# FNet mixing with a GeGLU feed-forward block: GpSimd's tensor work is given to VectorE

## The chip, the cores and the metric

The kernel runs on one core of one Trainium2 chip. The core has a tensor engine (PE, with a separate row PEld for the loading of weights), a vector engine (DVE, called VectorE or `V` in the code), a scalar engine (ACT, `A`), a general-purpose engine (POOL, GpSimd or `G`), and SP, whose queue issues all of this kernel's DMA transfers. Each engine executes its own instructions in the order in which they were written; semaphores make it wait for others. PE, DVE, ACT and POOL meet in SBUF; PE's results lie in PSUM banks. The metric is the device time of one execution in microseconds; less is better. Durations below come from one profiled execution.

## The reference

With tokens S = 2048, width D = 448 and inner width DF = 1792, all in float32:

```python
a = einsum("bsd,ed->bse", layernorm(x), dft_hid_re)
b = einsum("bsd,ed->bse", layernorm(x), dft_hid_im)
h = x + einsum("ts,bse->bte", dft_seq_re, a) - einsum("ts,bse->bte", dft_seq_im, b)
g = einsum("bsd,df->bsf", layernorm(h), w_gate)
u = einsum("bsd,df->bsf", layernorm(h), w_up)
out = h + einsum("bsf,fd->bsd", gelu(g) * u, w_down)
```

The layernorms have no affine part (eps 1e-5), the gelu is the tanh approximation.

## The kernel before

**Numbers in halves.** PE works in float16. Every operand is split into a hi part (made by ACT, `hi_part`, L108) and a lo part, the rest that hi leaves (made by DVE, `lo_part`, L112 and L114). A product takes several float16 matmuls. Many of the matrix products are Strassen-like: seven products of sums and differences of quarter blocks instead of eight. The sums of quarters (`..._sums`) are side work for DVE or POOL, and each result then gets its hi and lo part.

**Stages.** The sequence transform takes 64 steps; in steps 32 to 63 it is done by seven products ("fast", from about 175 to 333 us). In between, the hidden transform and the weights are prepared. Then the feed-forward block runs over three blocks of tokens: block 0 with 1024 tokens (14 tiles t = 0 to 13, about 334 to 460 us, "the gate/up block" below), and blocks 1 and 2 with 512 tokens each (tiles 14 to 41, 460 to 663 us), into which the down projection is woven (`dn_mm`). A tail of down products follows (663 to 695 us). A tile is one pair of quarter columns of gate and up: 38 matmuls of 512 columns in block 0, of 256 columns later.

**One gate/up tile** (class `GateUp`) has seven products in the banks X, Y, Z. Their names in the profile: `m` is a scaled copy of Z, `u` one of Y, `g` the gelu of X (all by ACT). DVE's `plus` (L1179) adds `u` to Z and gives `c` (c12 in the code); a second `plus` (L1179) adds `m` to Y and writes one half of `hs`, the hidden tile. Only then may PE add the last product y3 into Y. y3 of tile t is issued after the first two products of tile t+1, so that DVE has this long to do c and hs of tile t. From Y after y3, DVE makes the other half of `hs` by a product with `g` (L1248). ACT applies the gelu to `c` (L1261), and POOL multiplies that into the first half of `hs` (L1263, the gated product). Then SP stores `hs` (L1269) into a DRAM tile (`hid_dram`), from where the down projection loads it again as `hid` (L1286). `hs` has two buffers. In block 0 the sums of such loads are `dn_s` (L1333 to L1335), their hi and lo parts `dn_w`.

**Side work by slots.** Everything else in the gate/up block (gate/up weights for later tiles, the weights of down, normalised tokens for blocks 1 and 2) is hung on numbered slots: three per step of the sequence transform, then eight per tile from slot 192 on. `do(q)` emits what the tables put on slot q, at that place in the order of all engines. The tables: `W_AT` (gate/up weights: load, sums, hi, lo, store), `P_AT` (hidden transform and the moments of h), `F_AT` and `H_AT` (norms, sums, hi, lo and transposes of h), `T_AT` (sums of the transform's operands), `D_AT` (weights of down: load, sums, hi, lo in two pieces). A number in a table thus sets which instruction of DVE stands ahead of which. `gu_w` and `gw` are gate/up weights; their store into DRAM is L400, their load L1277; `wd` is a tile of down's weights, `wd_s` its five sums (L232 to L235, POOL), `xs` and `tt` belong to the normalised tokens, `hops` to their transposed form (SP's DMA transposes, L327).

**POOL's other work.** After each pair of token tiles of h, `ffn_rstd` refines a reciprocal square root: DVE's reciprocal, then five small steps on POOL (L213 to L217); `ffn_bias` has one more (L240) for four tiles. When a pair of token tiles is done in the down projection, class `Drain` adds PE's banks into `hr`: three adds straight from PSUM by DVE (L1111) and eight sums (L1139) with copies `v` made by ACT (L1107). In the loop these sums are given to DVE, in the tail (drains 5 and 6) they take the default engine, POOL. The last drain adds from PSUM (L1588) and its stores end the kernel.

Of the kernel before, what the change touches and what calls it, by code (L numbers as in the profile page):

```python
# [11 lines left out]
ALU = mybir.AluOpType  # L12

P = 128
S, D, DF = 2048, 448, 1792
# [7 lines left out]
EPS = 1e-5  # L23


X_SC = 16.0
# [6 lines left out]
def kernel(  # L33
# [173 lines left out]
    def ffn_rstd(q, j):  # L207
        tag = f"h{q}_{j}"
        mv = moments[q, j]
        sd = root(mv, tag, D)  # L210
        r = const.tile([P, 4, 2], F32, tag=f"r_{tag}", name=f"r_{tag}")
        V.reciprocal(r[:, 0], sd)
        G.tensor_scalar(r[:, 1], mv[:, :, 1], D * EPS, -0.5 / (D * X_SC**2), op0=ALU.add, op1=ALU.mult)  # L213
        G.tensor_mul(r[:, 2], r[:, 0], r[:, 0])
        G.tensor_mul(r[:, 2], r[:, 2], r[:, 1])
        G.tensor_scalar(r[:, 2], r[:, 2], 1.5, None, op0=ALU.add)
        G.tensor_mul(r[:, 3], r[:, 2], r[:, 0])  # L217
        moments[q, j] = mv, r[:, 3]


# [7 lines left out]
    def down_sums(n):  # L228
        t = wd32[n]
        place = (late, "dn_s") if n > 1 else (fops, "xs")  # L230
        s = wd_s[n] = place[0].tile([P, 5, HD], F32, tag=place[1], name=f"wd_s_{n}")
        G.tensor_sub(s[:, 2:4], t[:, 0:2], t[:, 2:4])  # L232
        t22 = t.rearrange("p (a b) d -> p a b d", a=2)
        G.tensor_add(s[:, 0:2], t22[:, :, 0], t22[:, :, 1])
        G.tensor_add(s[:, 4], t[:, 0], t[:, 3])  # L235

    def ffn_bias(q, j):
        mv, r = moments[q, j]
        if q < 2:
            G.tensor_mul(mv[:, :, 1], mv[:, :, 0], r)  # L240
            return
        sign = -1.0 if (q, j) == (NB - 1, 1) else 1.0
        V.scalar_tensor_tensor(mv[:, :, 1], mv[:, :, 0], sign, r, op0=ALU.mult, op1=ALU.mult)
# [537 lines left out]
    def h_store(q, j):  # L781
# [3 lines left out]
    gu, gw = {}, {}  # L785
    W_AT = {
# [14 lines left out]
    }  # L801
    P_AT = {
# [7 lines left out]
    }  # L810
    F_AT = {
# [4 lines left out]
    }  # L816
    T_AT = {
        6: (41, 46, 48),
        7: (48, 50, 54),
        0: (50, 54, 54),  # L820
        1: (57, 61, 63),
        2: (68, 92, 94),
        3: (67, 92, 93),
        4: (65, 68, 70),
        5: (69, 72, 72),
    }
    H_AT = {
# [4 lines left out]
    }  # L832
    D_AT = {
# [259 lines left out]
    class Drain:  # L1093
# [27 lines left out]
        def bank3(self):  # L1121
            self.add(3, 6, 1.0)

        def sums(self, parts, E=G):
            x11, x12, x21, x22 = self.x
            M3, M4, M2, M5 = self.v
            ops = (
                (E.tensor_add, x12, M3),
                (E.tensor_sub, x21, M4),
                (E.tensor_add, x21, M2),  # L1130
                (E.tensor_add, x12, M5),
                (E.tensor_sub, x11, M4),
                (E.tensor_add, x22, M3),
                (E.tensor_sub, x11, M5),
                (E.tensor_sub, x22, M2),
            )
            for k in parts:
                op, x, m = ops[k]
                op(x, x, m)  # L1139
# [46 lines left out]
    class GateUp:  # L1186
# [58 lines left out]
        def y3(self):  # L1245
            self.mul(self.Y, "A22", "T4", False)
            h, y, g = self.hidden(0), self.cols(self.Y), self.cols(self.g1)
            V.scalar_tensor_tensor(h, y, SC, g, op0=ALU.mult, op1=ALU.mult)  # L1248

        def cols(self, a):  # L1250
            return a.rearrange("p (n t) -> p n t", t=P)
# [7 lines left out]

        def c_last(self):  # L1260
            A.activation(self.c12, self.c12, AF.Gelu_apprx_tanh, scale=1.0 / H_SC)  # L1261
            c22 = self.hidden(1)
            G.tensor_mul(c22, c22, self.cols(self.c12))  # L1263

        def store(self):

# [146 lines left out]
    for t in range(NF):  # L1413
# [46 lines left out]
        if t == 3:  # L1460
            mv = moments[NB - 1, 1]
# [190 lines left out]
```

## Time and profile before

| | |
|---|---|
| time, median of 3 runs | 697.32 us (696.77 to 698.31) |
| profiled execution | 697.04 us, of which span 695.2 us, granted clock 1.000 |
| PE | 687.0 us busy, 99% of the span |
| DVE | 575.9 us, 83%, 1203 instructions |
| ACT | 416.9 us, 60% |
| POOL | 113.8 us, 16%, 127 instructions |
| gate/up block, 392 to 452 us | DVE 52.07 of 60 us, ACT 42.76, POOL 25.60 |

A row of a group reads: line, engine, operation, output<-inputs, shapes, how often | busy us in total, mean ns of one | idle time of the engine just before, and what ended it. A row of waits reads: who waited at which line <- for whom: us in total, how often, the longest. A row of the timeline reads: start, duration in us, engine, line, operation, count, and in brackets the idle time before it with what ended it; several like instructions in a row are put together. Idle time of an engine other than PE costs nothing by itself, unless PE waits behind it.

### The profile page before, as it was taken

How to read it: one execution, taken by the hardware profiler on the slowest of the kernel's cores; microseconds unless marked ns; L12 is line 12 of the kernel's file. 1: busy time of each engine (PE TensorE's matmuls, PEld its weight loads, DVE VectorE, ACT ScalarE, POOL GpSimd, SP SyncE). 2: the span in 40 equal slices, each digit the busy share in tenths (PEclk: the TensorE clock that was granted, in tenths of full speed). 3: DMA queues.
4: the chain of work that ended last, by engine and by line, in shares of the span. 5: the costliest groups of instructions: out<-in, count | busy, mean ns of one | idle time of the engine just before them, and what ended most of it. 6: DMA issues, size and time to landing. Idle time of an engine off the chain costs nothing.

```text
span 695.2 us, 13978 instructions
## 1 busy us (share of the span) xinstructions
PE 687.0 (99%) x5266; PEld 509.4 (73%) x5266; DVE 575.9 (83%) x1203; ACT 416.9 (60%) x855; POOL 113.8 (16%) x127
## 2 busy tenths in 40 slices
PE   9999999999999999999999999999999999999998
PEld 5555555555979889987644444459999999999997
DVE  7999799879999898995548997867788876899786
ACT  5777665957766655555536867655555453655631
POOL 0000001010011001000033443511020111233224
DMA  8778659879957649583655679697989985787612
GB/s 288 251 226 283 158 208 253 294 203 293 225 184 182 188 114 207 173 217 141 159 196 189 230 261 291 202 307 245 258 225 288 295 286 184 294 300 276 242 47 81
DMA packets 115781, 155.43 MB, mean 224 GB/s; under 512 B 63744, under 2 KB 80256, under 8 KB 115712
## 3 DMA queue, kind: packets, MB, share of 16 engines
q1 hardware_dynamic: 115712, 154.53, 73.3%
q8 instruction: 41, 0.67, 0.4%
q14 instruction: 28, 0.23, 0.1%
HBM read 105.74 MB, written 34.34 MB: 201 GB/s over the span
## 4 chain that ended last, share of the span: by engine, by line
PE 91%; DVE 3%; DMA 3%; ACT 1%; issue 1%; SPq 0%; DVEq 0%; ACTq 0%
PE acc L682 21%; PE acc_f L560 19%; PE acc_d L1373 15%; PE pY L1169 12%; PE y L768 9%; PE pZ L1169 8%; PE pX L1169 8%; DVE gu_w L114 1%; DMA hid_dram<-hs 1%; DMA gw<-w_dram 1%; ACT gu_w L108 0%; DMA x<-in_x_dram 0%; SPq L327 0%; ACT u L1225 0%; DVE hs L1179 0%
## 5 line engine op out<-in xcount | busy, mean ns | idle before, releaser
L1169 PEld LDWEIGHTS <-gw 128*128 128x128 f16 x1330 | 129.9, 98 | 44.1 <-issue 2.9
L682 PE MATMUL acc<-xs,ws 128*128 128x448 f16 x768 | 146.4, 352 | 0.1
L560 PEld LDWEIGHTS <-ws 128*128 128x128 f16 x1344 | 128.8, 98 | 1.6
L682 PEld LDWEIGHTS <-ws 128*128 128x128 f16 x768 | 75.1, 98 | 70.2 <-ACT ws L108 0.2
L1373 PE MATMUL acc_d<-wd,dn_w 128*128 128x224 f16 x1008 | 110.9, 259 | 1.7 <-DVE dn_w L112 1.7
L1373 PEld LDWEIGHTS <-dn_w 128*128 128x128 f16 x1008 | 96.7, 98 | 4.2 <-DVE dn_w L112 2.1
L1263 POOL TENSOR_TENSOR hs<-hs,c 128x256 f32<-128x256 f32 (+1 forms) x42 | 60.5, 1439 | 230.0 <-ACT c L1261 186.6
L560 PE MATMUL acc_f<-t,ws 128*128 128x224 f16 x768 | 91.9, 259 | 0.0
L1169 PE MATMUL pY<-hops,gw 128*128 128x256 f16 (+1 forms) x560 | 85.6, 294 | 1.9 <-DVE hs L1179 1.5
L114 DVE SCALAR_TENSOR_TENSOR ws<-wr,ws 128x768 f16<-128x768 f32 (+2 forms) x66 | 69.8, 1058 | 10.1 <-ACT ws L108 10.1
L560 PE MATMUL acc_f<-xs,ws 128*128 128x224 f16 x576 | 73.5, 259 | 0.0
L108 ACT ACTIVATE ws<-wr 128x768 f16<-128x768 f32 (+2 forms) x66 | 60.5, 916 | 10.2 <-DMA wr<-in_w_seq_dram 9.1
L768 PE MATMUL y<-wh,z 128*128 128x448 f16 x336 | 66.2, 352 | 0.0
L1169 PE MATMUL pX<-hops,gw 128*128 128x256 f16 (+1 forms) x385 | 61.7, 294 | 0.0
L1169 PE MATMUL pZ<-hops,gw 128*128 128x256 f16 (+1 forms) x385 | 61.7, 294 | 0.0
L768 PEld LDWEIGHTS <-z 128*128 128x128 f16 x336 | 32.9, 98 | 29.3
L1179 DVE SCALAR_TENSOR_TENSOR c<-pZ,u 128x256 f32<-128x256 f32 (+1 forms) x42 | 21.4, 508 | 36.6 <-ACT dn_w L108 17.7
L1214 ACT ACTIVATE pY<-pX 128x256 f32<-128x256 f32 (+1 forms) x42 | 18.4, 439 | 53.9 <-PE pX L1169 50.4
L108 ACT ACTIVATE ws<-sums 128x512 f16<-128x512 f32 x64 | 38.5, 623 | 18.6 <-DVE sums L510 14.2
L1169 PEld LDWEIGHTS <-gu_w 128*128 128x128 f16 x266 | 25.9, 98 | 31.3 <-issue 0.3
L1225 ACT ACTIVATE u<-pY 128x256 f32<-128x256 f32 (+1 forms) x42 | 19.0, 454 | 45.0 <-PE pY L1169 44.7
L112 DVE TENSOR_TENSOR dn_w<-dn_s,dn_w 128x640 f16<-128x640 f32 x48 | 42.0, 874 | 1.6 <-ACT dn_w L108 1.6
(160 smaller groups left out, 980.0 us busy)
## 6 DMA issues: line engine op xcount, KB each, us to landing
gw<-w_dram SPq DMA_DIRECT2D x35, 896.0 KB, 6.9
wr<-in_w_seq_dram SPq DMA_DIRECT2D x100, 256.0 KB, 4.3
hid_dram<-hs SPq DMA_DIRECT2D x27, 512.0 KB, 7.0
hid<-hid_dram SPq DMA_DIRECT2D x54, 256.0 KB, 5.3
w_dram<-gu_w SPq DMA_DIRECT2D x14, 896.0 KB, 4.8
wr<-in_w_seq_dram SPq DMA_DIRECT2D x14, 512.0 KB, 4.9
gu_raw<-in_w_gu_dram SPq DMA_DIRECT2D x14, 384.0 KB, 5.6
gu_raw<-in_w_gu_dram SPq DMA_DIRECT2D x14, 320.0 KB, 5.0
```

Source lines behind the costliest of these rows:

```text
L108: A.activation(dst, src, AF.Copy, scale=scale)
L112: V.tensor_sub(dst, src, hi)
L114: V.scalar_tensor_tensor(dst, src, scale, hi, op0=ALU.mult, op1=ALU.subtract)
L560: PE.matmul(fast_sum(n, k), fast_a(n, i, lw, a), fast_b(j, lx, b), start=j == 0 and m == 0 and k in (0, 1, 3, 5), stop=j == NT // 2 - 1 an ...
L682: PE.matmul(acc[key][:, :D], w[:, lw, block * P : (block + 1) * P], xs[c][:, lx, :], start=c == 0 and m == 0, stop=c == NT - 1 and m == 2,)
L768: PE.matmul(y[:, :D], z[p][:, lz, k, g * P : (g + 1) * P], wh[:, lw, k, :], start=p == NP - 1 and k == 0 and m == 0, stop=k == 6 and m == ...
L1169: PE.matmul(ps, w[:, wo, :], ops[:, OPS[b] + m, :], start=first and n == 0, stop=last and n == len(W_TERMS[a]) - 1, skip_group_check=True,)
L1179: V.scalar_tensor_tensor(dst, ps, SC, other, op0=ALU.mult, op1=ALU.add)
L1214: A.activation(self.Y, self.X, AF.Copy)
L1225: A.activation(self.u2, self.Y, AF.Copy, scale=SC)
L1263: G.tensor_mul(c22, c22, self.cols(self.c12))
L1373: PE.matmul(ps, w[:, la, a, :], wd[n][:, lb, b, :], start=n == 0 and m == 0 and opens, stop=n == NC - 1 and m == 2, skip_group_check=True,)
```

## The change

Five kinds of work leave POOL for DVE: the gated product, which now stands in `y3` behind the product with `g` (L1249 in the changed code; it stood in `c_last`); the three sums of each tile of down's weights; the small steps of `ffn_rstd`, of which two are now one; the product in `ffn_bias`; and the drain sums of the tail. POOL keeps the memsets and the identity matrix. The tables get other numbers at some places. One line less at L216 shifts all later lines by one.

```diff
@@ ffn_rstd
-        G.tensor_scalar(r[:, 1], mv[:, :, 1], D * EPS, -0.5 / (D * X_SC**2), op0=ALU.add, op1=ALU.mult)
-        G.tensor_mul(r[:, 2], r[:, 0], r[:, 0])
-        G.tensor_mul(r[:, 2], r[:, 2], r[:, 1])
-        G.tensor_scalar(r[:, 2], r[:, 2], 1.5, None, op0=ALU.add)
-        G.tensor_mul(r[:, 3], r[:, 2], r[:, 0])
+        V.tensor_scalar(r[:, 1], mv[:, :, 1], D * EPS, -0.5 / (D * X_SC**2), op0=ALU.add, op1=ALU.mult)
+        V.tensor_mul(r[:, 2], r[:, 0], r[:, 0])
+        V.tensor_mul(r[:, 2], r[:, 2], r[:, 1])
+        V.scalar_tensor_tensor(r[:, 3], r[:, 2], 1.5, r[:, 0], op0=ALU.add, op1=ALU.mult)
@@ down_sums
-        G.tensor_sub(s[:, 2:4], t[:, 0:2], t[:, 2:4])
+        V.tensor_sub(s[:, 2:4], t[:, 0:2], t[:, 2:4])
...
-        G.tensor_add(s[:, 0:2], t22[:, :, 0], t22[:, :, 1])
-        G.tensor_add(s[:, 4], t[:, 0], t[:, 3])
+        V.tensor_add(s[:, 0:2], t22[:, :, 0], t22[:, :, 1])
+        V.tensor_add(s[:, 4], t[:, 0], t[:, 3])
@@ ffn_bias
-            G.tensor_mul(mv[:, :, 1], mv[:, :, 0], r)
+            V.tensor_mul(mv[:, :, 1], mv[:, :, 0], r)
@@ tables
-        11: (1, 37, 46, 48, 51, 51, 51, 54, 54, 58),
+        11: (1, 39, 48, 48, 51, 51, 51, 54, 54, 58),
...
-        0: (49, 45, 51, 58, 61, 62, 64),
-        1: (62, 60, 66, 68, 73, 75, 76),
+        0: (50, 46, 52, 59, 61, 62, 64),
+        1: (62, 60, 66, 70, 75, 77, 76),
...
-        5: (259, 260, 268, 273, 273, 274, 276, 276, 281, 284, 284, 289, 285, 289, 285, 293),
+        5: (253, 254, 262, 267, 267, 268, 270, 270, 281, 284, 284, 289, 285, 289, 285, 293),
...
-        0: (192, 195, 203, 204, 203, 206, 206),
-        1: (187, 213, 217, 217, 218, 221, 221),
-        2: (207, 229, 233, 233, 234, 237, 237),
-        3: (223, 245, 249, 249, 250, 253, 253),
+        0: (184, 197, 203, 204, 201, 207, 207),
+        1: (187, 215, 219, 219, 220, 223, 226),
+        2: (206, 228, 232, 232, 233, 236, 237),
+        3: (229, 245, 249, 250, 251, 254, 254),
...
@@ Drain
-        def sums(self, parts, E=G):
+        def sums(self, parts, E=V):
@@ GateUp.y3
             V.scalar_tensor_tensor(h, y, SC, g, op0=ALU.mult, op1=ALU.mult)
+            c22 = self.hidden(1)
+            V.tensor_mul(c22, c22, self.cols(self.c12))
@@ GateUp.c_last
             A.activation(self.c12, self.c12, AF.Gelu_apprx_tanh, scale=1.0 / H_SC)
-            c22 = self.hidden(1)
-            G.tensor_mul(c22, c22, self.cols(self.c12))
```

How this moves instructions is shown at three places of the gate/up block. First, DVE from the moments of h's last token tile (L205) to hs of tile 3, before:

```order
L205 BN_AGGR mv_h_1_4512<-st_h_1_1_4606 128x2
L1248 SCALAR_TENSOR_TENSOR hs_4572<-pY_4474,g_2_4557 128x4x128
L114 SCALAR_TENSOR_TENSOR wd_4261<-wd_1_4166,wd_4261 128x448
L1179 SCALAR_TENSOR_TENSOR c_3_4651<-pZ_4597,u_3_4631 128x512
L1179 SCALAR_TENSOR_TENSOR hs_4653<-pY_4582,m_3_4603 128x4x128
L114 SCALAR_TENSOR_TENSOR wd_4261<-wd_s_4593,wd_4261 128x448
L114 SCALAR_TENSOR_TENSOR wd_4261<-wd_s_4593,wd_4261 128x672
```

The same engine and stretch in the changed kernel:

```order
L205 BN_AGGR mv_h_1_4504<-st_h_1_1_4594 128x2
L231 TENSOR_TENSOR wd_s_4604<-wd_1_4162 128x448
L233 TENSOR_TENSOR wd_s_4604<-wd_1_4162 128x448
L234 TENSOR_TENSOR wd_s_4604<-wd_1_4162 128x224
L1247 SCALAR_TENSOR_TENSOR hs_4565<-pY_4466,g_2_4550 128x4x128
L1249 TENSOR_TENSOR hs_4565<-hs_4565,c_2_4563 128x4x128
L1178 SCALAR_TENSOR_TENSOR c_3_4641<-pZ_4585,u_3_4624 128x512
L114 SCALAR_TENSOR_TENSOR wd_4256<-wd_1_4162,wd_4256 128x448
L1178 SCALAR_TENSOR_TENSOR hs_4645<-pY_4574,m_3_4591 128x4x128
```

The three sums of wd1 and the gated product of tile 2 are new there; `c_3` now stands ahead of the first lo part of wd1, and of the other two lo parts the last (672 columns) follows a tile later. On ACT, in the same stretch, `g_3` and the hi part of wd1 (448 columns) change places, before:

```order
L129 ACTIVATE sd_h_last<-mv_h_1_4512,eps_t 128x2
L1225 ACTIVATE u_3_4631<-pY_4582 128x512
L134 ACT_TABLE_LOAD
L134 ACTIVATE warm<-eps_t 128x1
L108 ACTIVATE wd_4261<-wd_1_4166 128x448
L1230 ACTIVATE g_3_4642<-pX_4581 128x512
```

The same engine and stretch in the changed kernel:

```order
L129 ACTIVATE sd_h_last<-mv_h_1_4504,eps_t 128x2
L1224 ACTIVATE u_3_4624<-pY_4574 128x512
L134 ACT_TABLE_LOAD
L134 ACTIVATE warm<-eps_t 128x1
L1229 ACTIVATE g_3_4633<-pX_4573 128x512
L108 ACTIVATE wd_4256<-wd_1_4162 128x448
```

Second, DVE between hs of tile 4 and the next product with `g`, where a weight's lo parts (`gu_w`) stand, before:

```order
L1179 SCALAR_TENSOR_TENSOR hs_4739<-pY_4663,m_4_4678 128x4x128
L263 TENSOR_TENSOR tt_0_4746<-xn_h_0_4728 128x192
L114 SCALAR_TENSOR_TENSOR gu_w_4710<-gu_s_4698,gu_w_4710 128x384
L114 SCALAR_TENSOR_TENSOR gu_w_4710<-gu_s_4698,gu_w_4710 64x3x128
L114 SCALAR_TENSOR_TENSOR gu_w_4710<-gu_s_4698,gu_w_4710 64x128
L114 SCALAR_TENSOR_TENSOR gu_w_4710<-gu_s_4698,gu_w_4710 128x256
L265 TENSOR_TENSOR tt_0_4746<-xn_h_0_4728 128x192
L266 TENSOR_TENSOR tt_0_4746<-xn_h_0_4728,tt_0_4746 128x192
```

The same engine and stretch in the changed kernel:

```order
L1178 SCALAR_TENSOR_TENSOR hs_4730<-pY_4655,m_4_4668 128x4x128
L231 TENSOR_TENSOR wd_s_4737<-wd_2_4513 128x448
L233 TENSOR_TENSOR wd_s_4737<-wd_2_4513 128x448
L234 TENSOR_TENSOR wd_s_4737<-wd_2_4513 128x224
L262 TENSOR_TENSOR tt_0_4741<-xn_h_0_4719 128x192
L114 SCALAR_TENSOR_TENSOR gu_w_4700<-gu_s_4688,gu_w_4700 128x384
L114 SCALAR_TENSOR_TENSOR gu_w_4700<-gu_s_4688,gu_w_4700 64x3x128
L114 SCALAR_TENSOR_TENSOR gu_w_4700<-gu_s_4688,gu_w_4700 64x128
L114 SCALAR_TENSOR_TENSOR gu_w_4700<-gu_s_4688,gu_w_4700 128x256
L264 TENSOR_TENSOR tt_0_4741<-xn_h_0_4719 128x192
L265 TENSOR_TENSOR tt_0_4741<-xn_h_0_4719,tt_0_4741 128x192
```

The three sums of wd2 are put in ahead of the weight's lo parts; before, they ran on POOL meanwhile. Third, DVE at tile 10, from hs of that tile to c of the next, before:

```order
L1179 SCALAR_TENSOR_TENSOR hs_5222<-pY_5148,m_10_5163 128x4x128
L268 TENSOR_TENSOR tt_1_5143<-xn_h_1_5070,tt_1_5143 128x192
L114 SCALAR_TENSOR_TENSOR gu_w_5189<-gu_s_5175,gu_w_5189 128x384
L114 SCALAR_TENSOR_TENSOR gu_w_5189<-gu_s_5175,gu_w_5189 64x3x128
L114 SCALAR_TENSOR_TENSOR gu_w_5189<-gu_s_5175,gu_w_5189 64x128
L114 SCALAR_TENSOR_TENSOR gu_w_5189<-gu_s_5175,gu_w_5189 128x256
L1248 SCALAR_TENSOR_TENSOR hs_5222<-pY_5148,g_10_5205 128x4x128
L114 SCALAR_TENSOR_TENSOR wd_4265<-wd_5_5010,wd_4265 128x448
L1179 SCALAR_TENSOR_TENSOR c_11_5295<-pZ_5251,u_11_5275 128x512
```

The same engine and stretch in the changed kernel:

```order
L1178 SCALAR_TENSOR_TENSOR hs_5219<-pY_5148,m_10_5163 128x4x128
L114 SCALAR_TENSOR_TENSOR gu_w_5194<-gu_s_5180,gu_w_5194 128x384
L114 SCALAR_TENSOR_TENSOR gu_w_5194<-gu_s_5180,gu_w_5194 64x3x128
L114 SCALAR_TENSOR_TENSOR gu_w_5194<-gu_s_5180,gu_w_5194 64x128
L114 SCALAR_TENSOR_TENSOR gu_w_5194<-gu_s_5180,gu_w_5194 128x256
L231 TENSOR_TENSOR wd_s_5239<-wd_5_5006 128x448
L233 TENSOR_TENSOR wd_s_5239<-wd_5_5006 128x448
L234 TENSOR_TENSOR wd_s_5239<-wd_5_5006 128x224
L1247 SCALAR_TENSOR_TENSOR hs_5219<-pY_5148,g_10_5204 128x4x128
L1249 TENSOR_TENSOR hs_5219<-hs_5219,c_10_5217 128x4x128
L114 SCALAR_TENSOR_TENSOR wd_4260<-wd_5_5006,wd_4260 128x448
L1178 SCALAR_TENSOR_TENSOR c_11_5288<-pZ_5243,u_11_5268 128x512
```

Here the sums of wd5 stand behind the weight's lo parts, the gated product behind the product with `g`, and the step of `tt` has gone to an earlier tile with the rest of its group (`H_AT`, row 5). On SP, the weight's store follows these lo parts, and hs's store now follows DVE's gated product (L1249) instead of POOL's.

More of the change, by code (lines that the diff above doesn't have):

```diff
@@ L802 @@
     P_AT = {
[2 rows of a table removed]
[2 rows of a table added]
         2: (77, 76, 82, 88, 94, 102, 97),
[4 rows of a table removed]
[4 rows of a table added]
     }
     F_AT = {
[4 rows of a table removed]
[4 rows of a table added]
     }
     T_AT = {
[L818 to L822, printed above, removed]
+        6: (41, 46, 51),
+        7: (48, 51, 55),
+        0: (50, 52, 54),
+        1: (59, 63, 65),
+        2: (65, 89, 95),
         3: (67, 92, 93),
```

20 rows, old and new, of tables (F_AT, H_AT, P_AT) are left out of this document.

## The prediction

> **What bounds the kernel now.** I read the page first, then PE's waits, then busy time by stage, then the timeline around each wait.
>
> ```profile
> PE 687.0 (99%) x5266; PEld 509.4 (73%) x5266; DVE 575.9 (83%) x1203; ACT 416.9 (60%) x855; POOL 113.8 (16%) x127
> PE 91%; DVE 3%; DMA 3%; ACT 1%; issue 1%; SPq 0%; DVEq 0%; ACTq 0%
> ```
>
> PE sets the time: 687.0 of 695.2 us. The change touches no matmul, so it can win only what PE now loses by waiting, and can lose by new waits of PE. PE's waits:
>
> ```profile
> PE acc_d L1373 <- DVE dn_w L112: 1.7, 1, 1.7
> PE pY L1169 <- DVE hs L1179: 1.5, 2, 1.0
> PE pw L102 <- POOL sign_t L93: 1.4, 1, 1.4
> PE pY L1169 <- ACT u L1225: 0.4, 1, 0.4
> PE acc_d L1373 <- ACT v L1107: 0.2, 1, 0.2
> L1169 PE MATMUL pY<-hops,gw 128*128 128x512 f16 x112 | 27.6, 379 | 1.9 <-DVE hs L1179 1.5 <-ACT u L1225 0.4
> ```
>
> The memset wait (1.4) opens the kernel and stays; the wait for v (0.2) follows an ACT wait that the change leaves. Four stops remain: 1.7, 1.5 in two, 0.4, together 3.6 us. A stop costs more than its row: a 512-wide matmul's record lasts 0.379 us, but 39 of them fill 8.00 us (448 to 456 in the next fence), 0.21 each, so each stop also exposes about 0.17. Four stops: 3.6 + 0.7 = **4.3 us**. That is what can be won.
>
> By stage (columns: length, then PE, PEld, DVE, ACT, POOL busy, clock, DMA share, GB/s):
>
> ```profile
> 392.00:452.00 60.00, 58.98 (x275) 26.64 (x273) 52.07 (x92) 42.76 (x82) 25.60 (x20) 1.00 0.82 260
> 436.00:440.00 4.00, 4.00 (x20) 1.84 (x19) 3.94 (x7) 2.94 (x8) 2.29 (x2) 1.00 0.00 0
> 448.00:456.00 8.00, 8.00 (x39) 3.63 (x37) 6.18 (x10) 4.45 (x7) 4.06 (x4) 1.00 1.04 337
> 470.00:663.00 193.00, 193.00 (x1874) 181.30 (x1872) 157.31 (x402) 103.72 (x257) 37.74 (x27) 1.00 0.80 261
> ```
>
> In the gate/up block DVE is 87% busy (52.07 of 60), where PE needs one DVE result per tile: hs of L1179, queued behind side work. With down interleaved (470 to 663) PE never stops.
>
> **The price of what moves.** Groups of instructions by line, POOL's first (the last two: shortest/median/longest in ns):
>
> ```profile
> L1263 POOL TENSOR_TENSOR hs<-hs,c 128x256 f32<-128x256 f32 x28 | 38.5, 1376 | 162.1 <-ACT c L1261 131.8 <-DVE dn_s L1335 15.5 <-DVE hs L1179 10.8
> L1263 POOL TENSOR_TENSOR hs<-hs,c 128x512 f32<-128x512 f32 x14 | 21.9, 1566 | 67.9 <-ACT c L1261 54.8 <-DVE hs L1179 12.6 <-DVE wd L114 0.5
> L1139 POOL TENSOR_TENSOR hr<-hr,v 128x224 f32<-128x224 f32 x16 | 12.4, 798 | 11.9 <-ACT v L1107 11.0 <-DVE hr L1111 0.6
> L510 DVE TENSOR_TENSOR sums<-wr 128x512 f32<-128x512 f32 x32 | 21.8, 682 | 4.1 <-DMA wr<-in_w_seq_dram 4.1
> L112 DVE TENSOR_TENSOR xs<-xf,xs 128x448 f16<-128x448 f32 x14 | 8.7, 618 | 0.2 <-ACT xf L431 0.2
> L1139 DVE TENSOR_TENSOR hr<-hr,v 128x224 f32<-128x224 f32 x40 | 14.6, 402 | 0.1
> L422 DVE SCALAR_TENSOR_TENSOR r_x<-r_x 128x1 f32<-128x1 f32 x16 | 3.5, 219 | 0.6
> L1333 DVE TENSOR_TENSOR dn_s<-hid x54: 404/415/951, 454.6 to 673.8; 128x256 f32<-128x256 f32 x54
> L1179 DVE SCALAR_TENSOR_TENSOR c<-pZ,u x27: 401/425/426, 474.2 to 660.7; 128x256 f32<-128x256 f32 x27
> ```
>
> On DVE a gated product costs 0.68 us in block 0 (14 of them, by L510) and 0.42 later (28, by L1333's median); one weight tile's three sums 2 x 0.62 + 0.40 = 1.63 (7 times); a drain sum 0.40 (16); the root's four small steps about 0.2 each (L422), 0.8, 7 times, and four bias products at 0.2. Gross: 9.5 + 11.8 + 11.4 + 6.4 + 5.6 + 0.8 = 45.5 us.
>
> Against it stands what POOL costs DVE now. The same four lo parts of a gate/up weight (L114), without POOL and with it:
>
> ```profile
> 185.91 1.77 DVE L114 SCALAR_TENSOR_TENSOR gu_w<-gu_s,gu_w 128x384 f16<-128x384 f32 x4
> 386.95 0.36 DVE L263 TENSOR_TENSOR tt<-xn_h 128x192 f32<-128x192 f32 x1 [0.43 <-ACT xn_h L252]
> 387.23 4.51 DVE L114 SCALAR_TENSOR_TENSOR gu_w<-gu_s,gu_w 128x384 f16<-128x384 f32 x4
> 391.66 0.81 DVE L265 TENSOR_TENSOR tt<-xn_h 128x192 f32<-128x192 f32 x1
> 387.57 1.33 POOL L1263 TENSOR_TENSOR hs<-hs,c 128x512 f32<-128x512 f32 x1 [7.60 <-ACT c L1261]
> 391.41 0.84 POOL L235 TENSOR_TENSOR wd_s<-wd 128x224 f32<-128x224 f32 x1
> ```
>
> 2.74 us lost on the four, and 0.45 on the next (0.81 against 0.36): 3.2 us, while POOL ran four operations without a gap from 387.57 to 392.25, 4.7 us. That is 0.68 us of DVE per POOL microsecond. An operation that reads PSUM isn't slowed: all c of L1179 lie within 0.401 and 0.426, while L1333, with both inputs in SBUF, goes from 0.404 up to 0.951. The Trainium skill, SBUF — State Buffer, "Who interferes with whom", says that a VectorE instruction with two SBUF inputs contends with a GpSimd instruction that reads SBUF, and one with at most one SBUF input does not. The trace agrees (0.951 and 0.426 at the longest).
>
> Bounds for 392–452: POOL is busy 25.60 us there, which at 0.68 is a loss of 17 on DVE, and nil if the loss at 387 had another cause. Part of DVE's queue reads PSUM, and DVE idles for 7.9 us, so I take half, 8.5. Added there: 60/8.2 tiles (38 matmuls of 0.21 or 0.22 a tile) x 0.68 = 5.0, and four weight tiles x 1.63 = 6.5. DVE goes from 52.1 to 55.1 of 60: it fits, and the relief falls where the work is added. From 470 to 663 it goes from 157 to 169 of 193 even without relief:
>
> ```profile
> L1179 DVE SCALAR_TENSOR_TENSOR c<-pZ,u 128x256 f32<-128x256 f32 x28 | 11.8, 421 | 30.0 <-ACT dn_w L108 17.7 <-PE pZ L1169 10.8 <-ACT xs L108 1.4
> ```
>
> DVE idles 30.0/28 = 1.07 us per tile ahead of c, which covers 0.42, so nothing changes for PE; without that cover it would cost up to 28 x 0.42 = 11.8. In the earlier stages the roots add 0.8 at a time, in front of weight parts that are ready about a step ahead; I cost them at nothing, at most 0.3 each if that lead is gone.
>
> **The four stops, one by one.**
>
> ```profile
> 367.75 4.50 DVE L114 SCALAR_TENSOR_TENSOR gu_w<-gu_s,gu_w 128x384 f16<-128x384 f32 x4
> 373.70 0.30 ACT L129 ACTIVATE sd_h_last<-mv_h,eps_t 128x2 f32<-128x2 f32 x1 [2.61 <-DVE mv_h L205]
> 376.49 0.63 DVE L114 SCALAR_TENSOR_TENSOR wd<-wd,wd 128x448 f16<-128x448 f32 x1 [2.25 <-ACT wd L108]
> ```
>
> *u, 0.4 (tile 3).* ACT waits 2.61 us for DVE's moments, then makes u. DVE was late by 4.50 − 1.77 = 2.73. With POOL silent the moments come 2.7 earlier; the three new sums (1.63) stand behind them. Gone: −0.4 − 0.17.
>
> *hs, 0.44 of the 1.5 (tile 3).* c and hs stood behind the lo part of wd1, which waited 2.25 for ACT's hi part. The new order puts c ahead of that lo part, and ACT is 2.6 earlier: −0.44 − 0.17.
>
> *hs, 1.02 (tile 5).* Between hs of tiles 4 and 5 DVE wins back the 3.2 us above and gets 1.63 and 0.68 more. Net −0.9 by full durations, about −1.2 as records back to back overlap (at 687.98 below four fill 1.28, 0.32 each, against 0.40). The wait is 1.02, so it goes and leaves a lead of a few tenths at most: the tightest place of the change. −1.02 − 0.17.
>
> *dn_w, 1.7.* This one is a chain over SP:
>
> ```profile
> SPq L400 <- DVE gu_w L114: 8.3, 1, 8.3
> 436.93 3.69 DVE L114 SCALAR_TENSOR_TENSOR gu_w<-gu_s,gu_w 128x384 f16<-128x384 f32 x4
> 440.68 0.33 SPq L400 DMA_DIRECT2D w_dram<-gu_w  x1
> 459.95 0.53 SPq L1269 DMA_DIRECT2D hid_dram<-hs  x1
> 468.20 0.42 DVE L1179 SCALAR_TENSOR_TENSOR hs<-pY,m 128x256 f32<-128x256 f32 x1 [2.39 <-DMA hid_dram<-hs]
> ```
>
> hs of tile 14 reuses the buffer of tile 12, whose store SP issued only at 459.95, behind transposes and loads that SP reached late, having stood 8.3 us for the weight store that DVE's slowed lo parts released at 440.68. Meanwhile the DMA engines idled (436–440: share 0.00). Without POOL these lo parts (3.69 there) save 1.9, and xs work now done a tile earlier a little more, so the queue starts over 2 us earlier and the store lands before DVE asks. Gone: −1.7 − 0.17. The store of each hs waits for the gated product, 0.68 on DVE now against 1.57 on POOL.
>
> *New waits.* A seed (L749) on ACT follows a hidden product that is one slot later, with its successor unmoved:
>
> ```profile
> 101.91 0.55 ACT L749 ACTIVATE y<-hx 128x448 f32<-128x448 f32 x1
> ```
>
> I take 0.1 for it, at most 0.3. In the tail, 16 sums come to DVE:
>
> ```profile
> 680.39 0.88 DVE L1333 TENSOR_TENSOR dn_s<-hs 128x256 f32<-128x256 f32 x1
> 687.98 1.28 DVE L1588 SCALAR_TENSOR_TENSOR hr<-acc_d,hr 128x224 f32<-128x224 f32 x4 [2.27 <-PE acc_d L1373]
> ```
>
> Back to back, as at 687.98, they take 16 x 0.32 = 5.1. DVE idles 2.27 before 687.98 and wins back some 3 (0.88 against 0.42 at each of six such sums and about the same at the lo parts), so the sums end about when PE delivers; +0.1, and at most +1.1 (by 0.40 each).
>
> **Sum.** 697.04 (the profiled execution; 695.2 of span and 1.84 around it) − 4.3 + 0.2 = 692.9. The median of the runs lies 0.28 above the profiled one: **693.2 us**. Best case all gone and nothing new, 692.7; PE's own work forbids more than some 0.3 below that.
>
> **Rivals.**
>
> *The dn_w stop stays (20%, 695.1).* For it: from 448 on the DMA share is 1.04; if the queue is bound by bandwidth, an earlier start is eaten by what lies ahead. Against it: 4 us of idle before. Price: 1.87 back.
>
> *New stops replace the old (16%, about 697).* DVE runs in order, and at the tiles with sums it gets 1.63 + 0.68 = 2.3 at once, while the longest wait for hs now is 1.02. If POOL's slow-down fell mostly on work that had slack, a net addition of up to 1.0 at four of them makes up the 3.6 us again.
>
> *DVE becomes the bound of the gate/up block (12%, slower, 701).* If relief is nil, DVE needs 52.1 + 5.0 + 6.5 = 63.6 us in a window of 60: 3.6 us of new stops, and none of the old ones gone: 697.3 + 3.6. It decides from a relief under 3.6 us on. Against it stand 4.51 and 1.77. The Trainium skill, Perfetto Trace Analysis, "Optimizing Scalar/DVE Operations", speaks against the change: when VectorE is saturated, moving work off to ScalarE or even GpSimd may make sense. It adds that GpSimd and VectorE share an SBUF read port, so that a move between those two might not help, and the 3.2 us above agrees with that half. By its first half alone the time would be this case's 701.
>
> *It does not do what it says.* All POOL rows named above leave POOL, which keeps memsets and the identity; I give it nothing.
>
> **How the numbers follow.** Forecast, all four stops gone: 52%, with its own range 692.4 to 694.8. A measurement tells 0.2%, 1.4 us, from no change: faster is under 695.9, slower over 698.7. Faster: 52 + 20 = 72%. Same: 16%. Slower: 12%. The range for 8 in 10 takes in both first cases and half of the third: 692.2 to 697.6.
>
> **What would show it.** In the changed profile: POOL without tensor work; the four lo parts back at about 1.8 us near 367, 387 and 437; PE's waits down to 1.4 (memset), 0.2 and a few tenths; no DVE wait for hid_dram, and L400's last store before 439; DVE's busy time between 583 (575.9 + 45.5, less half of 0.68 x 113.8) and 621 (no relief). Wrong it would be if hs (L1178 there) again heads PE's waits at tiles 4 to 13, or if dn_w still does.

## The result, and the profile after

The changed kernel takes 693.57 us (median of 6 runs, 693.18 to 693.99) against 697.47 for the kernel before on the same chip (6 runs): a ratio of 0.9937, 95% interval 0.9916 to 0.9957, thus 0.4 to 0.8% faster. Forecast were 693.2 us, range 692.2 to 697.6. The span of the profiled execution fell from 695.2 to 692.1 us.

The page of the changed kernel, busy times and the chain that ended last:

```profile
PE 687.2 (99%) x5266; PEld 510.2 (74%) x5266; DVE 581.3 (84%) x1314; ACT 416.9 (60%) x855; POOL 0.9 (0%) x9
PE 97%; DMA 1%; ACT 1%; issue 1%; SPq 0%; POOL 0%; DVE 0%; POOLq 0%
```

DVE took over everything POOL did and is busy only 5.4 us longer (575.9 before). The chain now runs over PE for 97% of the span, before for 91%. What is left of PE's waits:

```profile
PE pw L102 <- POOL sign_t L93: 1.4, 1, 1.4
PE y L767 <- DMA z<-zs: 0.3, 1, 0.3
PE acc_d L1372 <- ACT v L1106: 0.2, 1, 0.2
```

All four stops of the prediction (dn_w, hs twice, u) are gone, and a small one, for the transposes of z, is new. By stage (columns as in the prediction):

```profile
392.00:452.00 60.00, 60.00 (x279) 27.20 (x278) 53.17 (x109) 41.48 (x79) 0.00 (x0) 1.00 0.87 278
470.00:663.00 193.00, 193.00 (x1876) 181.48 (x1874) 157.19 (x427) 102.56 (x255) 0.00 (x0) 1.00 0.78 257
```

PE has no idle time in either. DVE's load between 392 and 452 rose by 1.1 us only (52.07 before), although 11.5 us of work were added there, and from 470 to 663 it did not rise at all (157.31 before). What the moved work costs on DVE, by groups:

```profile
L1249 DVE TENSOR_TENSOR hs<-hs,c 128x256 f32<-128x256 f32 x28 | 11.6, 413 | 0.0
L1249 DVE TENSOR_TENSOR hs<-hs,c 128x512 f32<-128x512 f32 x14 | 9.5, 680 | 0.0
L231 DVE TENSOR_TENSOR wd_s<-wd 128x448 f32<-128x448 f32 x7 | 4.3, 614 | 0.0
```

Of what POOL had slowed, first the sums of `dn_s` (shortest/median/longest in ns), then a row of the timeline (start, duration in us):

```profile
L1332 DVE TENSOR_TENSOR dn_s<-hid x54: 412/416/426, 452.3 to 671.1; 128x256 f32<-128x256 f32 x54
```

```profile
388.12 1.80 DVE L114 SCALAR_TENSOR_TENSOR gu_w<-gu_s,gu_w 128x384 f16<-128x384 f32 x4
```

A gated product takes 0.68 or 0.41 us, as priced. The longest of the 54 first sums of `dn_s` takes 0.426 us (0.951 before), and the four lo parts of a weight take 1.80 us (4.51 before).

### The profile page after: what moved, and what is told of

Read it like the earlier page. It is cut to its first block, busy times and chain, and to the rows that moved or that the text cites. A ratio compares the mean times of both kernels' runs of the same rounds, so it can differ in the third digit from the quotient of the medians.

```text
span 692.1 us, 13916 instructions
## 1 busy us (share of the span) xinstructions
PE 687.2 (99%) x5266; PEld 510.2 (74%) x5266; DVE 581.3 (84%) x1314; ACT 416.9 (60%) x855; POOL 0.9 (0%) x9
## 4 chain that ended last, share of the span: by engine, by line
PE 97%; DMA 1%; ACT 1%; issue 1%; SPq 0%; POOL 0%; DVE 0%; POOLq 0%
PE acc L681 21%; PE acc_f L559 18%; PE acc_d L1372 16%; PE pY L1168 14%; PE pX L1168 10%; PE pZ L1168 10%; PE y L767 9%; DMA z<-zs 1%; PE pw L102 1%; SPq L706 0%; ACT dn_w L108 0%; ACT v L1106 0%; ACT hx L756 0%; ACT y L758 0%; ACT y L748 0%
## 5 line engine op out<-in xcount | busy, mean ns | idle before, releaser
L112 DVE TENSOR_TENSOR dn_w<-dn_s,dn_w 128x640 f16<-128x640 f32 x48 | 39.2, 818 | 1.8 <-ACT dn_w L108 1.8
L108 ACT ACTIVATE dn_w<-dn_s 128x640 f16<-128x640 f32 x48 | 34.9, 727 | 7.9 <-DVE dn_s L1334 7.8
```

The costliest lines, as they stand in the source:

```text
L108: A.activation(dst, src, AF.Copy, scale=scale)
L112: V.tensor_sub(dst, src, hi)
```

## The experiments

Two theories of the prediction stood against each other first: that POOL's reads of SBUF slow DVE and this makes the stops (A), and that the new numbers in the tables, thus another order, removed them (B). The kernel before ran beside every experiment and took 698.3 to 698.7 us (medians) on those chips, so ratios to it are compared; the change itself stands at 0.9937. Where ratios don't tell two kernels apart, PE's waits in the traces are compared. A loss "from start to start" is by how much the starts of two neighbouring groups of matmuls lie further apart than without a stop; it also shows what a matmul's record hides.

### The tables alone

```diff
-(tables W_AT to D_AT of the kernel before)
+(the same tables of the changed kernel)
 (every engine as in the kernel before)
```

> The tables of the changed kernel, with all of GpSimd's work left on GpSimd as before. Theory A (GpSimd's reads of SBUF slow VectorE, and that is where the stops come from): the stop for hs at tile 5 (1.0) and the one for dn_w (1.7) stay; the 0.44 at tile 3 goes, since c and g no longer stand behind wd1; a stop of about 0.5 near 276 us comes, as in the changed kernel: 696.5 to 698 us, four lo parts still over 3.5 us near 367, 387 and 437. Theory B (the order in the tables removed the stops): 693.5 to 694.5, with no PE wait for hs or dn_w.

Measured: 698.9 us, ratio 1.0005 (0.9988 to 1.0022): no gain. PE's waits:

```profile
PE pY L1169 <- DVE hs L1179: 1.7, 2, 1.4
PE acc_d L1373 <- DVE dn_w L112: 1.5, 1, 1.5
PE pY L1169 <- ACT u L1225: 0.4, 1, 0.4
```

They are nearly those of the kernel before. The 0.44 at tile 3, expected to go, stayed (start to start 0.49 lost at 378), and the longer hs stop sits at tile 4 (387) now. The four lo parts near 368 and 437 last 4.50 and 4.51 us, those near 389 only 2.77, less than the 3.5 that theory A expected. The stop that was expected at 276 did not come, although the new tables were there. The order by itself brings nothing while POOL works: theory B in its plain form has fallen.

### The engines alone

```diff
-(tables W_AT to D_AT of the changed kernel)
+(the same tables of the kernel before)
 (every engine as in the changed kernel)
```

> The engines of the changed kernel with the tables of the kernel before. Theory A: u at tile 3, hs at tile 5 and dn_w go; the 0.44 at tile 3 may stay (c stands behind the first lo part of wd1 again); no stop near 276: 693 to 694.5 us. Theory B: the stops for hs and dn_w come back, as the added VectorE work stands at places that were not made for it: 696 to 699 us.

Measured: 705.08 us, ratio 1.0091 (1.0065 to 1.0118): slower, further than either theory had it. PE's waits; then, in the timeline at the largest, SP's issue and DVE:

```profile
PE pY L1168 <- DVE hs L1178: 5.1, 2, 5.0
PE y L767 <- ACT y L748: 1.5, 2, 0.9
PE acc_f L559 <- DVE ws L114: 1.1, 3, 0.4
PE acc_d L1372 <- DVE dn_w L112: 0.9, 1, 0.9
```

```profile
347.20 0.49 SPq L225 DMA_DIRECT2D wd<-in_w_down_dram  x1
351.73 0.62 DVE L231 TENSOR_TENSOR wd_s<-wd 128x448 f32<-128x448 f32 x1 [4.74 <-DMA wd<-in_w_down_dram]
353.11 0.69 DVE L1178 SCALAR_TENSOR_TENSOR hs<-pY,m 128x512 f32<-128x512 f32 x1
```

The first weight tile of down is loaded at 347.20, behind other transfers on SP's queue. DVE reaches its sums at once and stands 4.74 us, with hs of tile 0 queued behind them; PE waits 5.0 us for that hs. In the kernel before POOL stood at the same place for longer, and nobody noticed:

```profile
POOL wd_s L232 <- DMA wd<-in_w_down_dram: 15.9, 1, 15.9
```

The stop at tile 5 and the wait for u did go, and of the 0.44 at tile 3 some 0.14 is left from start to start (the second hs wait, 0.18, is a new one at tile 10). But dn_w, which theory A expected to go, fell only from 1.7 to 0.9. So theory A holds for u and hs and for dn_w in part, and moving work onto an engine that runs in order also moves its waits there.

### The engines, with that one load early

```diff
 (every engine as in the changed kernel, tables of the kernel before)
-        0: (192, 195, 203, 204, 203, 206, 206),
+        0: (184, 197, 203, 204, 201, 207, 207),
```

> Engines of the changed kernel, tables of the kernel before, except the row for tile 0 of down's weights (load at slot 184 instead of 192). Theory: the 5 us stop at tile 0 comes from VectorE standing in order behind sums that wait for this load; with the load early it goes whole: 700 us (705.1 less 5.1), the other stops (1.5 for y of the hidden transform, 1.1 for ws, 0.9 for dn_w) stay. Rival: the stop comes from the added time of the sums, and only the part that was the wait's excess goes: 702 to 704 us.

Measured: 698.42 us, ratio 0.9994 (0.9981 to 1.0007), less than the 700 that was expected. The whole stop went and a little more: the span is 697.3 against 703.1 us, 5.8 less. What is left of PE's waits, beside the 1.4 for the memset, 0.2 for hs and 0.2 for v, are these three:

```profile
PE y L767 <- ACT y L748: 2.2, 2, 1.3
PE acc_f L559 <- DVE ws L114: 1.1, 3, 0.4
PE acc_d L1372 <- DVE dn_w L112: 0.8, 1, 0.8
```

The wait for y has the same form as the one just removed. ACT (two rows) and DVE (one) in the timeline around one of the two waits, of 0.90 us at 208:

```profile
205.14 1.41 ACT L251 ACTIVATE xn_h<-hx,mv_h,r_h 128x448 f32<-128x448 f32 x2 [1.87 <-DVE mv_h L239]
208.09 0.55 ACT L748 ACTIVATE y<-hx 128x448 f32<-128x448 f32 x1
204.95 0.15 DVE L239 TENSOR_TENSOR mv_h<-mv_h,r_h 128x2 f32<-128x2 f32 x1
```

The bias product takes 0.15 us on DVE, but it comes after the lo parts of `ws`, and ACT, which waits 1.87 us for it, has the next seed (L748) queued behind, on which PE waits. In the changed kernel's tables the seed comes ahead of the norm, L748 before L251.

### Useless reads on POOL

```diff
@@ GateUp.c_last
             A.activation(self.c12, self.c12, AF.Gelu_apprx_tanh, scale=1.0 / H_SC)
+            G.tensor_mul(self.m5, self.c12, self.c12)
@@ down_sums
         V.tensor_add(s[:, 4], t[:, 0], t[:, 3])
+        two = prev.m5[:, : 2 * HD].rearrange("p (a d) -> p a d", a=2)
+        G.tensor_sub(two, t[:, 0:2], t[:, 2:4])
+        G.tensor_add(two, t22[:, :, 0], t22[:, :, 1])
+        G.tensor_add(two[:, 0], t[:, 0], t[:, 3])
```

> The changed kernel, and beside it GpSimd does again as much as before, to no purpose: one product of c with itself per tile where the gated product stood, and three sums of down's weights per weight tile, results into a dead tile. Nobody waits for them. Theory A: VectorE's two-input operations become slow again although it now has the moved work as well: 53.2 us of 60 between 392 and 452 become 62 to 70, and PE gets 2 to 8 us of waits for hs and dn_w: 696 to 702 us. Theory C (what counted was GpSimd's late result, not its reads): no change, 693.6 us.

Measured: 705.04 us, ratio 1.0085 (1.0055 to 1.0115), 3 us above the range of theory A. The page's busy times, the stage from 392 to 452, and PE's waits:

```profile
PE 688.8 (98%) x5266; PEld 509.8 (72%) x5266; DVE 611.7 (87%) x1314; ACT 416.7 (59%) x855; POOL 82.7 (12%) x72
```

```profile
392.00:452.00 60.00, 56.31 (x259) 25.12 (x258) 59.14 (x103) 39.06 (x75) 20.43 (x16) 1.00 0.73 233
```

```profile
PE pY L1172 <- DVE hs L1182: 7.6, 7, 1.9
PE acc_d L1377 <- DVE dn_w L112: 1.6, 1, 1.6
```

The same 1314 DVE instructions as in the change last 30.4 us longer (611.7 against 581.3) because POOL reads beside them for 82.7 us, 0.37 us lost per POOL microsecond. DVE is full between 392 and 452, and PE stops at seven tiles. Nobody waits for these results, so it isn't their lateness: theory C has fallen.

### Useless writes on POOL

```diff
@@ GateUp.c_last
             A.activation(self.c12, self.c12, AF.Gelu_apprx_tanh, scale=1.0 / H_SC)
+            G.tensor_mul(self.m5[:, :1], self.c12[:, :1], self.c12[:, :1])
+            for _ in range(3):
+                G.memset(self.m5, 1.0)
@@ down_sums
         V.tensor_add(s[:, 4], t[:, 0], t[:, 3])
+        G.tensor_add(prev.m5[:, :1], t[:, 0, :1], t[:, 3, :1])
+        for _ in range(6):
+            G.memset(prev.m5, 1.0)
```

> As the run with useless products, but GpSimd only writes: per place one 128x1 operation that reads SBUF, then memsets of 128x512 (three per gate/up tile, six per weight tile) into the dead tile. Theory A in the form that two inputs in SBUF meet GpSimd's reads: VectorE keeps its times (four lo parts 1.8 us) and the time stays at 693.6. Rival: any GpSimd access to SBUF slows VectorE: as in the run with products, 696 to 702 us.

Measured: 694.06 us, ratio 0.9927 (0.9906 to 0.9948), as the change. The page's busy times and the lo parts in the timeline:

```profile
PE 687.4 (99%) x5266; PEld 510.2 (74%) x5266; DVE 582.1 (84%) x1314; ACT 417.1 (60%) x855; POOL 105.6 (15%) x226
```

```profile
388.23 1.80 DVE L114 SCALAR_TENSOR_TENSOR gu_w<-gu_s,gu_w 128x384 f16<-128x384 f32 x4
```

POOL is busy 105.6 us, nearly as long as in the kernel before: 70.2 us with memsets and 34.5 with the 49 operations on a single column. DVE takes 582.1 us against 581.3 and the lo parts stay at 1.80. It is POOL's reading of whole tiles that slows DVE, not its being busy or its writing. The Trainium skill, SBUF — State Buffer, "Who interferes with whom", says that a VectorE instruction with two SBUF inputs contends with a GpSimd instruction that reads SBUF and not with one that only writes it; this pair of runs (611.7 and 582.1) agrees.

### One part of the change undone at a time

The gated product back on POOL, the rest as changed:

```diff
@@ GateUp.y3
-            c22 = self.hidden(1)
-            V.tensor_mul(c22, c22, self.cols(self.c12))
@@ GateUp.c_last
             A.activation(self.c12, self.c12, AF.Gelu_apprx_tanh, scale=1.0 / H_SC)
+            c22 = self.hidden(1)
+            G.tensor_mul(c22, c22, self.cols(self.c12))
```

> The changed kernel with the gated product alone back on GpSimd, at its old place. Theory A: its reads cost VectorE at most 0.68 x 1.57 = 1.1 us per tile of block 0 and save 0.6; in the changed kernel hs of tile 4 is ready just when PE wants it and hs of tile 5 some 0.5 us ahead, so stops of a few tenths to 1 us come back at tiles 4 and 5, and dn_w's may: 693.8 to 696 us. Theory B' (with the new order any engine will do): 693.6.

Measured: 693.49 us, ratio 0.9929 (0.9910 to 0.9947), as the change and as B' had it. PE has no wait for hs, u or dn_w; the stops that theory A expected at tiles 4 and 5 did not come. The page's busy times, and the lo parts in the timeline:

```profile
PE 686.9 (99%) x5266; PEld 509.6 (74%) x5266; DVE 584.9 (85%) x1272; ACT 417.2 (60%) x855; POOL 61.8 (9%) x51
```

```profile
368.32 2.73 DVE L114 SCALAR_TENSOR_TENSOR gu_w<-gu_s,gu_w 128x384 f16<-128x384 f32 x4
```

With 42 instructions fewer DVE is busy 3.6 us more (584.9 against 581.3), and the lo parts near 368 last 2.73 instead of 1.78, but PE doesn't wait: by the timeline hs ends 0.76, 0.39 and 0.35 us ahead of PE's y3 at tiles 3, 4 and 5 (1.15, 0.08 and 0.51 in the change). The product costs DVE some 1 us there and gives back its own 0.68. With the rest of the change in place, its largest item brings no time.

The sums of down's weights back on POOL, the rest as changed:

```diff
@@ down_sums
-        V.tensor_sub(s[:, 2:4], t[:, 0:2], t[:, 2:4])
+        G.tensor_sub(s[:, 2:4], t[:, 0:2], t[:, 2:4])
...
-        V.tensor_add(s[:, 0:2], t22[:, :, 0], t22[:, :, 1])
-        V.tensor_add(s[:, 4], t[:, 0], t[:, 3])
+        G.tensor_add(s[:, 0:2], t22[:, :, 0], t22[:, :, 1])
+        G.tensor_add(s[:, 4], t[:, 0], t[:, 3])
```

> The changed kernel with the three sums of each tile of down's weights alone back on GpSimd, at their new places. Theory A: GpSimd's 3.3 us per weight tile cost VectorE up to 2.2 us where they meet its lo parts, against 1.63 saved; the lead of 0.5 at tile 5 is about used up: 693.4 to 695 us, with the four lo parts near 387 at 3 to 4 us again. Theory B': 693.6, lo parts at 1.8.

Measured: 695.52 us, ratio 0.9949 (0.9933 to 0.9965), half a microsecond above theory A's range; the interval overlaps the change's, the stops are plain. PE's waits, then POOL and DVE in the timeline during tile 10:

```profile
PE acc_d L1372 <- DVE dn_w L112: 0.6, 1, 0.6
PE pY L1168 <- DVE hs L1178: 0.4, 1, 0.4
```

```profile
428.84 1.14 POOL L231 TENSOR_TENSOR wd_s<-wd 128x448 f32<-128x448 f32 x1 [13.66 <-ACT m L1219]
430.05 1.57 DVE L1249 TENSOR_TENSOR hs<-hs,c 128x512 f32<-128x512 f32 x1
431.54 1.01 DVE L356 TENSOR_TENSOR gu_s<-gu_raw 128x384 f32<-128x384 f32 x1
```

The stop isn't where it was expected: the lo parts near 387 and 437 kept 1.79 us. The sums met other operations, during tile 10 the gated product of tile 9 (1.57 instead of 0.68) and a weight's sum (1.01 instead of 0.55), and made hs of tile 10 late.

The small steps of the root and the bias products back on POOL:

```diff
@@ ffn_rstd, ffn_bias
-        V. (four steps, and the bias product)
+        G. (five steps, and the bias product, as in the kernel before)
```

> The changed kernel with the small steps of h's root and the bias products back on GpSimd, the rest as changed. They are short (0.3 to 0.6 us each) and no engine with slack used up waits at once: 693.4 to 693.9 us, no new stop of PE over 0.2. Rival (the two-input contention matters in the fast stage too, where VectorE is 95% busy): ws or y waits of 0.5 and more between 100 and 330 us, 694 to 695.

Measured: 694.1 us, ratio 0.9931 (0.9910 to 0.9953). The time is 0.2 us above the expected range and thus in the rival's, but the ratio is not told apart from the change's, and the trace has none of the rival's waits for ws or y (the 0.31 lost at 103 us is the change's own). And the drain sums of the tail back on POOL:

```diff
-        def sums(self, parts, E=V):
+        def sums(self, parts, E=G):
```

> The changed kernel with the drain sums of the tail alone back on GpSimd. Theory: they neither cost nor bring anything, since VectorE waits for PE at the end either way: 693.4 to 693.8 us; the six sums of dn_s after 663 at 0.7 to 0.9 us again instead of 0.3 to 0.4. Rival (they delay the last dn_w or the last adds): 694 or more, or under 693.

Measured: 694.08 us, ratio 0.9933 (0.9907 to 0.9958): again in the rival's range by the time, and not told apart from the change. The six sums of dn_s after 670 take 0.74 to 0.88 us again, as expected. DVE's wait before the last adds shows why that need not cost PE anything:

```profile
684.17 1.28 DVE L1587 SCALAR_TENSOR_TENSOR hr<-acc_d,hr 128x224 f32<-128x224 f32 x4 [2.20 <-PE acc_d L1372]
```

```profile
682.57 2.62 DVE L1138 TENSOR_TENSOR hr<-hr,v 128x224 f32<-128x224 f32 x8
```

The first row is of this experiment, the second of the change: there the eight sums fill the 2.2 us in which DVE waited for PE.

### Less slack on VectorE

```diff
             V.tensor_mul(c22, c22, self.cols(self.c12))
+            if self.block == 0:
+                V.tensor_mul(self.m5, self.c12, self.c12)
```

> The changed kernel with VectorE's gated product made twice in block 0 (the second into a dead tile): 14 x 0.6 us more, from 53.2 to 57.6 of 60 between 392 and 452. By the leads in the changed trace (hs of tile 4: 0.08, tile 5: 0.52, others 0.8 to 1.3) PE stops about 0.5 at tile 4, 0.1 to 0.5 at tile 5 and a few tenths for dn_w: 694 to 695.5 us. Rival (VectorE as the bound from 87% on): the stops add up over the tiles, 3 us and more: 697 or over.

Measured: 694.57 us, ratio 0.9941 (0.9925 to 0.9956). PE's one new wait, and the stage:

```profile
PE pY L1168 <- DVE hs L1178: 0.4, 1, 0.4
```

```profile
392.00:452.00 60.00, 60.00 (x279) 27.08 (x278) 57.31 (x117) 41.23 (x80) 0.00 (x0) 1.00 0.87 274
```

One stop of 0.4 us, at tile 4 (PE goes on at 387.16), with a loss of 0.17 from start to start at tile 5, as the leads of the changed trace said; dn_w, expected to cost a few tenths, did not stop. With DVE 96% busy (57.31 of 60) PE has no idle time in that window. A high busy share alone is not what makes PE wait here.

### The weight's store late, without POOL

```diff
-            lambda f=f: (gu[f].lo(False), gw.update({f: gu[f].w} if f in JIT_F else {})),
+            lambda f=f: ([V.tensor_mul(prev.m5, prev.g1, prev.g1) for _ in range(3 * (f == 12))], gu[f].lo(False), gw.update({f: gu[f].w} if f in JIT_F else {})),
```

> The changed kernel with three useless VectorE products (128x512, 0.6 us apart, into a dead tile) directly ahead of the last four lo parts of weight 12 at tile 10, so that this weight's store leaves about 1.8 us later, with no GpSimd work at all. In the changed kernel the store of hs of tile 12 landed at 464.0 and hs of tile 14 began at 464.6. Theory (the dn_w stop of 1.7 was SP's and the DMA queue's lateness after that weight's store): a dn_w stop of 0.7 to 1.5 us comes back, VectorE waits for hid_dram again: 694.3 to 695.3 us. Rival (the stop came from VectorE's own slow work near 460 to 469, or the queue makes the time up): no dn_w stop, 693.6 to 693.9.

Measured: 696.48 us, ratio 0.9967 (0.9950 to 0.9984). PE's new wait, then SP and DVE in the timeline:

```profile
PE acc_d L1372 <- DVE dn_w L112: 2.4, 1, 2.4
```

```profile
439.22 0.33 SPq L399 DMA_DIRECT2D w_dram<-gu_w  x1
458.69 0.53 SPq L1268 DMA_DIRECT2D hid_dram<-hs  x1
467.87 0.43 DVE L1178 SCALAR_TENSOR_TENSOR hs<-pY,m 128x256 f32<-128x256 f32 x1 [3.10 <-DMA hid_dram<-hs]
```

In the changed kernel the same two issues and the same instruction read:

```profile
436.80 0.33 SPq L399 DMA_DIRECT2D w_dram<-gu_w  x1
456.26 0.53 SPq L1268 DMA_DIRECT2D hid_dram<-hs  x1
464.63 0.42 DVE L1178 SCALAR_TENSOR_TENSOR hs<-pY,m 128x256 f32<-128x256 f32 x1
```

A weight's store 2.4 us later makes the store of hs of tile 12 2.4 us later, 19 us down the queue. That store also takes longer to land, 9.1 us against 7.8; less a lead of 0.6 in the change, this is DVE's wait of 3.1, and PE stops 2.4 us (that this equals the delay is chance). The dn_w stop is back, larger than expected (the time is 1.2 us above the range), with POOL silent and DVE's work near 460 untouched.

### Two table entries back

```diff
-        0: (50, 46, 52, 59, 61, 62, 64),
+        0: (50, 46, 52, 58, 61, 62, 64),
...
-        5: (153, 147, 152, 159, 170, 187, 173),
+        5: (147, 147, 152, 159, 170, 187, 173),
```

> The changed kernel with two table entries as before: the transposes of z for hidden pair 5 at slot 147 (not 153) and the first hidden product of pair 0 at slot 58 (not 59). Theory: these two moves made the two small stops that the changed kernel has and the kernel before had not (0.49 at 276 us, 0.31 at 103 us); they go, 692.8 to 693.1 us. Rival: the move of z's transposes made room for something else on SP's queue, and a stop of like size comes elsewhere: 693.4 to 694.

Measured: 693.27 us, ratio 0.9918 (0.9901 to 0.9936), the lowest of all, though not told apart from the change (0.9916 to 0.9957). Both small stops are gone from its trace; PE waits for the first memset (1.4) and for v (0.2) only. The stop at 276 was not the same in all runs with slot 153: 0.49 lost in the change, 0.35, 0.11 and none in others, so what remains to be had is some 0.3 to 0.8 us.

## Why the prediction was right, and where it was off

**What can be won.** Four stops of 3.6 us, 4.3 with what a matmul's record hides: all four went. New small stops take back 0.8, so 3.5 should be left; the spans of the profiled executions differ by 3.1, the medians by 3.9. The sum was right in sign and size.

**The price of the moved work.** 45.5 us were priced; by the groups after, it is 9.5 + 11.6 + 11.3 + 6.1 + 5.0 = 43.5. The relief follows: 575.9 + 43.5 − 581.3 = 38 us, or 0.33 per microsecond of POOL's 113.8, which is the half of 0.68 that was taken. DVE's 581.3 us lie just under the forecast of 583 to 621, as the gross price was a little high. Between 392 and 452 the relief was larger than the 8.5 that was taken: 11.5 us came in and DVE rose by 1.1, to 53.2 and not 55.1.

**u and hs at tile 3.** In the timeline of the changed kernel, ACT's wait for the moments is 0.20 us (2.61 before):

```profile
372.53 0.30 ACT L129 ACTIVATE sd_h_last<-mv_h,eps_t 128x2 f32<-128x2 f32 x1 [0.20 <-DVE mv_h L205]
376.61 0.68 DVE L1178 SCALAR_TENSOR_TENSOR hs<-pY,m 128x512 f32<-128x512 f32 x1
```

hs of tile 3 is ready over a microsecond ahead of PE (378.44). The prediction gave the new order and the earlier ACT as reasons together. The order alone removed nothing (it stayed with the tables alone), the engines alone left 0.14 of it.

**hs at tile 5.** It went, with 0.52 us to spare, the "few tenths" of the prediction. But "the tightest place" is tile 4, where hs is ready 0.08 us ahead, as little as before the change (0.05): there the last lo part of wd1 and the gated product are new. The prediction has no term for this tile, so that no stop came there was luck. The run with doubled products stopped at that tile first.

**dn_w.** The chain over SP was right, and the run that delayed the weight's store alone shows it. The store left at 436.80, before the 439 that the prediction set as its mark, and no DVE wait for hid_dram is left at hs. The store of hs of tile 12 leaves 3.7 us earlier than before; 1.7 of these are the stops at earlier tiles that are gone (hs of tile 10 begins at 434.34 against 436.06). A silent POOL alone is not enough: with the old tables and the load early dn_w still cost 0.8. There the store of hs of tile 12 left as soon after hs of tile 10 as in the change (22.0 and 21.9 us), but took 8.9 us to land, against 7.8 in the change and 8.1 before. So the rival with 20%, that the DMA queue eats part of the earlier start, came true in that run; in the change it did not, with the DMA share at 1.05 from 438 on in it too. What makes that transfer longer stays open.

**New waits.** The 0.1 for the seed was mis-sized: it measured 0.31 at 103 us, the upper end that was given. The stop of 0.49 at 276 stood in no term; the move of z's transposes on SP's queue was not weighed. The tail cost nothing, as said: the sums fill DVE's wait.

**The earlier stages.** "In front of weight parts that are ready about a step ahead; I cost them at nothing" gave the right number for a wrong reason. With the old tables the same steps cost 1.5 to 2.2 us of waits for y and 1.1 for ws. What keeps y free is the order: ACT's seeds ahead of its norms. That `ws` has no wait either must lie in the order too, since the engines are the same; which entry of the tables does it was not tested.

**The slower rival.** It was put on a busy DVE without relief, 701. The engines alone are slower, 1.0091, but by another mechanism: DVE stands in order behind a transfer (4.74 us) and ACT behind a 0.15 us product. With useless reads on POOL the rival came true as described (1.0085).

**Where the gain sits.** The parts don't add. Everything on POOL with the new tables: no gain. The gated product alone back on POOL: the full gain. The sums alone back: stops of 0.6 and 0.4. What made the stops for u and for hs at tile 5 is POOL's run of a product and three sums, 4.7 us long, which costs DVE 2.7 to 3.2 us within one tile; a lone product costs some 1 us, and most tiles have 0.8 to 1.3 us of lead. That reading fits all the runs, but no run has the product and the three sums on POOL and the rest on DVE.

## What to carry to other kernels

Count a second engine's cost not by its busy share but by what it does to the first: here 114 us on GpSimd cost VectorE 38 us, in clumps just where TensorE needed a result, while the same work on VectorE cost 43 us spread over places that could be chosen. Before work is moved onto an in-order engine, list what it waited for on the old one: GpSimd stood 15.9 us for a transfer at no cost, VectorE stood 4.7 us for the same transfer and TensorE stopped for 5. So the move and the new order belong together: the order alone brought nothing, and the move alone cost 0.9%.

## What the runs showed of the hardware

The slow-down depends on what GpSimd does with SBUF: 82.7 us of two-input products and sums cost VectorE 30.4 us, 105.6 us of memsets and operations on one column cost 0.8 us.

A long stop costs TensorE more than its length. After the stop of 4.96 us in the run with the engines alone, TensorE ran at half its clock for about 3 us (busy times by stretch; the column after the x's is the clock):

```profile
353.60:356.60 3.00, 2.75 (x7) 0.99 (x7) 1.84 (x5) 0.00 (x0) 0.00 (x0) 0.50 0.09 38
```

Seven matmuls fill 3.00 us there, 0.43 each instead of 0.21, so that stop cost 5.1 + 1.5 us; with the load early the span fell by 5.8, as the waits for y grew by 0.7. In the profiled execution of the run with the late store a stop of 2.4 us left the clock at 1.00. The Trainium skill, TensorE: Matmul & The Clock Gate, "Part 1: The HAM clock gate", puts the gap from which the array cools at about 3.4 us; these two stops lie on either side of it.

Stops of some 2 us may cost the clock in some executions all the same. Half the clock for 3 us makes a mean of 0.998 over some 700 us, which is what the run with the engines alone shows. Of the 52 executions of the kernel before beside the experiments, 22 have a mean of 0.998 or less and took 699.2 to 701.3 us, the other 30 took 697.2 to 698.8. With the late store it is four of ten (697.4 to 697.7 us against 695.0 to 696.7), and none of the six of the change. Where the clock fell in those executions, and how long their stops were, no trace shows.
